# Tile 2 transposed within contraction step 1, in two parts, and multiplied ahead of step 2

## The chip, the cores and the metric

The kernel runs on one core of one Trainium2 chip. The metric is the device time of one execution in microseconds (us). Every run in this document was of the fast state with a listed clock of 1.0; where two kernels are compared by a ratio, it is the mean time of one kernel's fast runs over that of the other's of the same rounds, so it is not quite the ratio of the medians that are quoted.

Engines are named as the profile names them: PE is TensorE's matmul side, PEld its weight loads, ACT is ScalarE, DVE is VectorE, POOL is GpSimd, SP issues most of the DMA transfers. PSUM (PS in the profile's lines) is the memory into which PE writes here; an eviction is the copy of a result out of it. A load lands when its last part has arrived, and a hole is a stretch in which PE has nothing to start.

## The reference, cut to what matters

The input is 2048 rows of 512 numbers. They are layer-normalized, and the result goes into two branches whose outputs are added to the input: a state space model and a gated feed-forward net. The change touches only the first matmuls of the second branch, for the first 512 rows.

```python
x = A_x                                  # (1, 2048, 512), bf16
xn = _layernorm(x, axis=-1)
return x + _A_ref(xn, ...) + _B_ref(xn, w_gate, w_up, w_down)

def _B_ref(x, w_gate, w_up, w_down):     # 512 -> 1376 -> 512
    return (_gelu(x @ w_gate) * (x @ w_up)) @ w_down
```

## The kernel before

The kernel is a list of operations, each with an engine, a modelled duration, and the tiles that it reads and writes. A static scheduler orders ACT, DVE and POOL from the model; PE and SP keep the order in which the program names their operations. The order on PE is therefore what the source says.

At the start nothing is on the chip, so the first 512 rows are worked off in the order in which data arrive. They form four tiles of 128 rows (0 to 3). Each is centred on DVE, transposed on PE in blocks of 128 columns into PSUM (`cent_T`), and evicted by ACT. The contraction over 512 columns has four steps (k = 0 to 3). Each step needs a slice of the gate weights and a slice of the up weights, which come as separate loads in the order of the steps, with the rows of tiles 2 and 3 between them. `ks(k, j, ...)` multiplies step k of tile j.

```python
def cent_T(j, k0, k1, bank, eng="A", c0=0):   # transpose blocks k0..k1 of tile j, then evict
    ...
    PE(f, 56.0 * (k1 - k0), [XNp[j][k0 > 0] if j < 2 else XN[j], IDN], [BANK[bank]], "T0")
    ...
def GT_k(k, j, u, ws, first=False):           # one matmul of step k, tile j, column group u
    ...
    PE(lambda e: e.matmul(dst, XCd(j, k), WGU[:, ws[0]:ws[-1] + 1, k, f0:f1], ...),
       ..., [(WGc, WUc)[w_][k] for w_ in ws] + [XCs[j][k > 0]] + ..., [BANK[bank]], "GK")
...
def ks(k, j, w_, first=False):
    for u in range(2):
        GT_k(k, j, u, w_, first)
...                                           # step 0 of tiles 0 and 1, their transposes
for j in range(2):
    ks(1, j, [0, 1])                          # step 1 of tiles 0 and 1
ch(*stats(0, 2)); ch(sub(2)); ...             # DVE: centre tile 2
...
cent_T(2, 0, 4, 7)                            # all of tile 2, one eviction
for j in range(2):
    ks(2, j, [0, 1])                          # step 2 of tiles 0 and 1
for k in range(3):
    ks(k, 2, [0, 1], k == 0)                  # steps 0, 1, 2 of tile 2
for j in range(3):
    ks(3, j, [0, 1])                          # step 3 of tiles 0, 1, 2
    ...
    if j == 0:
        cent_T(3, 0, 4, 6)
for (j, u), bank in zip([(3, 0), (3, 1), ...], ...):
    GT_mm(j, u, bank)                         # tile 3 over all steps, and the rest
```

## Time and profile before

| | before |
|---|---|
| time, first three runs | 177.21, 177.51, 178.35 us; median 177.51 us |
| span of the profiled execution | 175.7 us |
| PE busy | 172.1 us of it |
| idle PE just ahead of step 2 | 0.25 us (7.18 to 7.42) |
| tile 3's first matmul over all steps | 11.10 us |

From the page of before: the busy time of PE, and the shares of the chain that ended last.

```profile
PE 172.1 (98%) x868; PEld 84.0 (48%) x883; DVE 159.8 (91%) x279; ACT 95.5 (54%) x185; POOL 10.7 (6%) x24
...
PE 98%; issue 1%; DVE 0%
```

PE bounds the kernel from beginning to end. A busy share says little about what can be won; the starts of the matmuls say more. The timeline of PE in before, where the columns are start, time until the group ended, engine, line, operation, shapes and count (L679 are transposes, L700 the matmuls of single steps, L711 tile 3):

```profile
4.57 0.38 PE L700 MATMUL PS<-arena 128*128 128x256 bf16 x2
...
4.84 0.38 PE L700 MATMUL PS<-arena 128*128 128x256 bf16 x2
...
5.77 1.35 PE L700 MATMUL PS<-arena 128*128 128x256 bf16 x6
6.95 0.39 PE L679 MATMUL PS<-arena 128*128 128x128 bf16 x4
7.42 2.75 PE L700 MATMUL PS<-arena 128*128 128x512 bf16 x12
10.01 0.39 PE L679 MATMUL PS<-arena 128*128 128x128 bf16 x4
10.23 1.03 PE L700 MATMUL PS<-arena 128*128 128x512 bf16 x4
11.10 0.81 PE L711 MATMUL PS<-arena 128*128 128x512 bf16 x3
```

The end of a matmul in the profile reaches into the next one (one of 512 columns is shown as 0.38 us long, and the next starts 0.216 us after it), so holes have to be read from starts. Four transposes start at 6.95 and should have been followed by a matmul at 7.18 (four times 0.056 us); the next starts at 7.42. The trace has the landing of step 2's up slice at 7.29, and the matmul follows 0.135 us after it. That is the hole that the change aims at. From 7.42 on, matmuls of 512 columns start every 0.2157 us without a gap. Fifteen holes of exactly one matmul's length later in the trace are lost records: the page has 868 matmuls beside 883 weight loads.

One more line of before matters later. It is the view of one line's instructions (L700) between 4.4 and 6.4 us, with shortest, middle and longest duration in ns:

```profile
L700 PE MATMUL PS<-arena x10: 270/272/377, 4.6 to 6.3; 128*128 128x256 bf16 x8, 128*128 128x512 bf16 x2
```

A matmul of 256 columns takes about 0.27 us in this execution from its first real matmul on.

### The profile page before, as it was taken

What the parts mean: (1) busy time and instruction counts of PE and PEld (TensorE: products, weight loads), DVE (VectorE), ACT (ScalarE), POOL (GpSimd) and SP (SyncE); (2) the same over time, 40 slices, a digit from 0 to 9 for tenths busy, and PEclk for the clock granted to TensorE, in tenths of its full rate; (3) what the DMA queues carried; (4) which work ended last, traced back from release to release, by engine and by line L of the source; (5) the groups of instructions that cost most, each with busy time, mean ns of one, the idle gap of its engine ahead of it and who ended that gap; (6) DMA issues with size and microseconds to landing.
All of it is one profiled execution on the core that took longest, in us unless ns stands there. A gap on an engine that the chain in (4) does not pass through costs nothing.

```text
span 175.7 us, 2494 instructions
## 1 busy us (share of the span) xinstructions
PE 172.1 (98%) x868; PEld 84.0 (48%) x883; DVE 159.8 (91%) x279; ACT 95.5 (54%) x185; POOL 10.7 (6%) x24
## 2 busy tenths in 40 slices
PE   8999999999999999999999999999999999999995
PEld 3545564644544444444644444444464444444454
DVE  6987999996999989889899999989999899999941
ACT  5476677899876898383576792000667970000000
POOL 3122030201000000002100000000000000000000
DMA  5899999695998000002015000002001000000311
GB/s 155 241 320 174 215 178 222 126 132 113 191 298 225 0 4 2 0 30 85 8 39 111 1 0 0 4 0 90 30 0 30 4 0 0 0 0 0 120 64 60
DMA packets 32420, 14.36 MB, mean 82 GB/s; under 512 B 23736, under 2 KB 32408, under 8 KB 32408
## 3 DMA queue, kind: packets, MB, share of 16 engines
q1 hardware_dynamic: 32240, 14.07, 35.5%
q8 instruction: 7, 0.11, 0.3%
q10 hardware_dynamic: 168, 0.13, 0.2%
q14 instruction: 5, 0.04, 0.1%
HBM read 6.46 MB, written 2.10 MB: 49 GB/s over the span
## 4 chain that ended last, share of the span: by engine, by line
PE 98%; issue 1%; DVE 0%
PE PS L883 37%; PE PS L842 32%; PE PS L748 16%; PE PS L711 4%; PE PS L700 3%; PE PS L816 3%; PE PS L932 2%; PE PS L679 1%; PE PS L939 0%; DVE arena L901 0%
## 5 line engine op out<-in xcount | busy, mean ns | idle before, releaser
L883 PE MATMUL PS<-arena 128*128 128x512 bf16 (+3 forms) x317 | 65.9, 366 | 0.3
L842 PE MATMUL PS<-arena 128*128 128x512 bf16 x257 | 57.1, 379 | 0.4
L883 PEld LDWEIGHTS PS<-arena 128*128 128x128 bf16 (+1 forms) x323 | 30.8, 98 | 35.2
L842 PEld LDWEIGHTS PS<-arena 128*128 128x128 bf16 x264 | 25.8, 98 | 30.2
L786 DVE TENSOR_TENSOR_SCAN arena<-arena 128x512 bf16<-128x512 f32 x32 | 38.9, 1255 | 0.0
L857 ACT ACTIVATE arena<-PS 128x512 bf16<-128x512 f32 x33 | 19.8, 599 | 25.8 <-DVE arena L901 16.7
L748 PE MATMUL PS<-arena 128*128 128x512 bf16 (+1 forms) x134 | 28.0, 366 | 0.1
L861 ACT ACTIVATE arena<-PS 128x512 bf16<-128x512 f32 x33 | 19.8, 600 | 5.1 <-PE PS L842 5.1
L875 ACT ACTIVATE PS<-arena 128x512 f32<-128x512 bf16 (+2 forms) x17 | 9.6, 581 | 19.7 <-DVE arena L901 19.0
L748 PEld LDWEIGHTS PS<-arena 128*128 128x128 bf16 x136 | 13.3, 98 | 14.1
L757 ACT ACTIVATE arena<-PS 128x512 bf16<-128x512 f32 x32 | 17.7, 592 | 2.1 <-PE PS L748 2.1
L901 DVE TENSOR_TENSOR arena<-PS,arena 128x512 bf16<-128x512 f32 (+2 forms) x17 | 10.9, 653 | 6.4 <-PE PS L883 6.4
L863 DVE TENSOR_TENSOR arena<-arena 128x512 bf16<-128x512 bf16 x33 | 13.1, 416 | 1.7 <-ACT arena L861 1.6
L775 DVE TENSOR_TENSOR arena<-arena 128x4096 bf16<-128x4096 bf16 (+1 forms) x5 | 9.2, 1859 | 0.8 <-ACT arena L606 0.8
L773 DVE TENSOR_TENSOR arena<-arena 128x4096 bf16<-128x4096 bf16 (+1 forms) x5 | 9.2, 1859 | 0.1
L798 DVE TENSOR_TENSOR arena<-arena 128x4096 bf16<-128x4096 bf16 x4 | 9.2, 2288 | 0.1
L799 DVE TENSOR_TENSOR arena<-arena 128x4096 bf16<-128x4096 bf16 x4 | 9.1, 2284 | 0.0
L720 ACT ACTIVATE arena<-PS,arena 128x256 bf16<-128x256 f32 (+1 forms) x16 | 6.6, 448 | 3.9 <-PE PS L700 2.1
L610 DVE BATCH_NORM_STATS2 arena<-arena 128x6 f32<-128x512 bf16 x12 | 7.7, 679 | 0.1
L711 PE MATMUL PS<-arena 128*128 128x512 bf16 (+1 forms) x40 | 7.1, 336 | 0.0
L723 DVE SCALAR_TENSOR_TENSOR arena<-PS,arena 128x256 bf16<-128x256 f32 (+1 forms) x16 | 6.3, 445 | 0.5 <-PE PS L700 0.5
L700 PE MATMUL PS<-arena 128*128 128x512 bf16 (+1 forms) x28 | 6.2, 349 | 0.2
(96 smaller groups left out, 124.6 us busy)
## 6 DMA issues: line engine op xcount, KB each, us to landing
out_dram<-arena SPq DMA_DIRECT2D x15, 128.0 KB, 1.7
arena<-in_A_x_dram SPq DMA_DIRECT2D x3, 512.0 KB, 5.3
arena<-in_B_w_down_dram SPq DMA_DIRECT2D x1, 1280.0 KB, 7.2
arena<-in_B_w_gate_dram SPq DMA_DIRECT2D x4, 128.0 KB, 3.0
arena<-in_B_w_up_dram SPq DMA_DIRECT2D x4, 128.0 KB, 3.1
arena<-in_B_w_gate_dram SPq DMA_DIRECT2D x1, 480.0 KB, 6.5
arena<-in_B_w_up_dram SPq DMA_DIRECT2D x1, 480.0 KB, 7.4
arena<-arena SPq DMA_TRANSPOSE x25, 3.1
```

The source lines that it names most:

```text
L700: PE(lambda e: e.matmul(dst, XCd(j, k), WGU[:, ws[0]:ws[-1] + 1, k, f0:f1], start=first, stop=k == KD - 1, skip_group_check=True), d_pe([w ...
L711: ins_ = e.matmul(dst, XCd(j, k), WGU[:, :, k, f0:f1], start=(k == 0), stop=(k == KD - 1))
L748: ins_ = e.matmul(PS[bank][:, 128 * j0:128 * j1], BBT[c][dk].ap[:, 128 * s:128 * (s + 1)], XNT[b].ap[:, dk, 128 * j0:128 * j1], start=(dk ...
L757: GATE["evBu"] = ACT(lambda e, bank=bank, k3=k3, s=s, c=c: e.activation(SSc[k3][s][c].ap, PS[bank][:, :], ACTF.Copy), d_act(512), [BANK[ba ...
L786: V(lambda e, g=g, rb=rb, init=init: e.tensor_tensor_scan(g.ap, rb, g.ap, init, ALU.mult, ALU.add), d_dve_scan(512), [g, PA[RRr]] + ([CARc ...
L842: ins_ = e.matmul(PS[bank][0:m, c0:c1], W.ap[:, dk, 128 * ft:128 * ft + m], XNT[b].ap[:, dk, c0:c1], start=(dk == 0), stop=(dk == KD - 1))
L857: GATE["last_gelu"] = ACT(lambda e, bg=bg, kk=kk, m=m: e.activation(GG[kk].ap[0:m, :], PS[bg][0:m, :], ACTF.Gelu_apprx_tanh), d_act(512), ...
L861: ACT(lambda e, bu=bu, kk=kk, m=m: e.activation(UPB[kk].ap[0:m, :], PS[bu][0:m, :], ACTF.Copy), d_act(512), [BANK[bu]], [UPB[kk]], "evU")
L863: V(lambda e, kk=kk, m=m, ft=ft, k2=k2: e.tensor_tensor(HTt[k2][ft].ap[0:m, :], GG[kk].ap[0:m, :], UPB[kk].ap[0:m, :], ALU.mult), d_dve_tt ...
L875: ACT(lambda e: e.activation(PS[bank][:, c0:c1], X[tt].ap[:, c0:c1], ACTF.Copy), d_act(c1 - c0), [X[tt]], [BANK[bank]], "seed")
L883: ins_ = e.matmul(PS[bank][:, c0:c1], l_[:, 128 * j:128 * (j + 1)], r_[:, c0:c1], start=False, stop=last and n == len(ops) - 1, skip_group ...
L901: V(lambda e: e.tensor_tensor(OUTB[ko].ap[:, c0:c1], PS[bank][:, c0:c1], XD[tt].ap[:, c0:c1], ALU.add), d_dve_1x(c1 - c0), [BANK[bank], XD ...
```

## The change

The intent is to have something to multiply while step 2's weights are on their way. Tile 2 is transposed earlier, between step 1 of tile 0 and step 1 of tile 1, in one block and three, so that the first block is evicted early. Its steps 0 and 1, four matmuls of 0.2157 us or 0.86 us, then run ahead of step 2. The number of matmuls and transposes stays the same; one ACT eviction is added. The last two edits only exchange two PSUM banks for the transposes and matmuls of tile 3.

```diff
         ks(0, 1, [1])
-        for j in range(2):
-            ks(1, j, [0, 1])
-        ch(*stats(0, 2)); ch(sub(2)); ch(*stats(0, 0)); ch(*stats(0, 1))
+        ch(*stats(0, 2)); ch(sub(2))
+        ks(1, 0, [0, 1])
+        cent_T(2, 0, 1, 7)
+        cent_T(2, 1, 4, 6)
+        ks(1, 1, [0, 1])
+        ks(0, 2, [0, 1], True)
+        ch(*stats(0, 0)); ch(*stats(0, 1))
...
-        cent_T(2, 0, 4, 7)
-        for j in range(2):
+        ks(1, 2, [0, 1])
+        for j in range(3):
             ks(2, j, [0, 1])
-        for k in range(3):
-            ks(k, 2, [0, 1], k == 0)
...
-                cent_T(3, 0, 4, 6)
+                cent_T(3, 0, 4, 7)
...
-                                (7, 6, 0, 1, 2, 3, 4, 5, 0, 7)):
+                                (6, 7, 0, 1, 2, 3, 4, 5, 0, 7)):
```

## The prediction

> **What bounds the kernel.** TensorE. The page has it busy 172.1 of 175.7 us; the chain of waits is 98% PE. The timeline of PE starts shows no real gap after 7.42 us: matmuls follow every 0.216 us (512 columns) or 0.108 us (256)[...]. The 15 later holes of 0.216 us ("issue" in the chain) are lost records: 868 matmuls stand beside 883 weight loads, 15 apart. So only PE idle time before 7.5 us can be won.
>
> **That idle time.** Between the last fill matmul (4.24) and 7.42: 0.27 us (first eviction by DVE), 0.15 (eviction of tile 1's block 0), 0.07 (step 1's weights and an eviction), 0.02 (tile 1's second eviction), and 0.25 from 7.18 to 7.42: tile 2's transposes are done, and step 2 waits for its up-weight slice, which lands at 7.29 (landing to next matmul start: 0.135 us).
>
> **What the change does.** Matmul and transpose work is the same. Tile 2's transposes split into 1 + 3 blocks between tile 0's and tile 1's step 1; tile 2's steps 0 and 1 (four matmuls, 0.86 us) move ahead of step 2. Added: one ScalarE eviction (0.28 + 0.49 us in place of 0.60) at about 6.75 us, where ScalarE idles 0.9 us. DVE's order is chained and the same.
>
> Expected PE times:
> - step 1 of tile 0: 6.06 as now; transposes of tile 2 at 6.49 (its centred rows are ready at 6.19).
> - step 1 of tile 1: 6.71; tile 2 step 0: 7.14 (block evicted by about 7.08); tile 2 step 1: 7.58.
> - step 2 of three tiles: 8.01 to 9.31, without waiting: its weights landed at 7.29.
> - step 3: its up slice lands at 9.25, so the first matmul cannot start before 9.39. It would have been ready at 9.31; before, it started at 9.58. So 0.07 to 0.1 us of the win becomes a new wait here.
> - from then on the order is as before, 0.19 us earlier. Tile 3's eviction must end by about 10.85; ScalarE does the first gelu just ahead of it, so 0 to 0.05 us may be lost.
>
> Of the 0.27 us removed, about 0.15 to 0.19 us remains, all on the critical path. Nothing downstream has less slack: the second weight chunk lands 0.9 us, the first B matrix 0.7 us, the transposed tiles 0.7 to 0.8 us before their first matmul.
>
> **Predicted time.** 177.51 - 0.2 = 177.3 us; range 176.8 to 177.9, as the three runs of before spread over 1.1 us. Chances: faster by over 2% 0.01, within 2% 0.98, slower 0.01. With repeated rounds I expect a ratio of about 0.999.
>
> **What would show it.** The PE timeline: the 0.25 us hole before step 2 gone; step 3 starting within 0.15 us of its up slice's landing, with a wait on a DMA there; tile 3's first matmul at about 10.9 instead of 11.10 us; later work shifted by as much; matmul count unchanged but for lost records.
>
> **What would make it wrong.** (1) The landing of the step 3 slices moves from run to run; 0.2 us later, the win is nil, since before too would then sit on it; earlier, up to 0.27 us. (2) The kernel's static scheduler reorders ScalarE, DVE or GpSimd; that could open a PE wait later, which the chain would show. (3) The split eviction comes later than 7.14, if ScalarE is busy: a hole before tile 2's step 0 or 1.

## The result, and the profile after

The changed kernel took 177.5 us (median of six runs, 177.25 to 177.98), the kernel before 177.41 us (six runs, 177.21 to 178.35). The ratio is 1.000 with a 95% interval of 0.9975 to 1.0025. The time lies in the predicted range, but the predicted gain of 0.2 us is not to be seen: the interval is 0.44 us wide to each side, and a change without any effect would have met the range too.

The order of instructions on DVE, POOL and SP is the same in both programs; on ACT one eviction became two, and PE has the new order. So the static scheduler did not disturb anything else.

From the page of after, the same two lines:

```profile
PE 172.8 (98%) x868; PEld 84.5 (48%) x883; DVE 159.8 (91%) x279; ACT 95.6 (54%) x186; POOL 10.7 (6%) x24
...
PE 98%; issue 0%; DVE 0%
```

PE is busy 0.7 us longer, with the same number of matmuls. The span is 176.2 us, 0.5 us longer than in the profile of before. The timeline of PE in after shows where that comes from:

```profile
4.73 0.59 PE L700 MATMUL PS<-arena 128*128 128x256 bf16 x2
...
5.21 0.63 PE L700 MATMUL PS<-arena 128*128 128x256 bf16 x2
...
6.61 0.82 PE L700 MATMUL PS<-arena 128*128 128x256 bf16 x4
7.27 0.39 PE L679 MATMUL PS<-arena 128*128 128x128 bf16 x4
7.49 3.19 PE L700 MATMUL PS<-arena 128*128 128x512 bf16 x14
10.51 0.39 PE L679 MATMUL PS<-arena 128*128 128x128 bf16 x4
10.74 1.03 PE L700 MATMUL PS<-arena 128*128 128x512 bf16 x4
11.60 0.38 PE L711 MATMUL PS<-arena 128*128 128x512 bf16 x1
```

Two things are to be read here. First, the hole is gone: from step 1's first matmul (6.84, within the group of 6.61) to tile 3 (11.60) there is 4.76 us, which is just the work, 20 matmuls of 0.2157 us and 8 transposes of 0.0557 us. In before the same stretch took 5.04 us (6.06 to 11.10). (PE came later here; by the estimate under experiments 1 and 2 the old order would have had no hole at step 2 in this execution either.) Second, step 1 begins 0.78 us later than in before, although the code up to there is the same in both kernels. Of these, 0.16 us are there from the first transpose on (4.03 against 3.87 us; the first rows landed that much later, at 2.97 against 2.82 us). The rest comes after it: the first two pairs of matmuls took 0.59 and 0.63 us, against 0.38 us in before. The view of line L700 in after, between 4.4 and 6.4 us:

```profile
L700 PE MATMUL PS<-arena x6: 373/421/421, 4.7 to 6.2; 128*128 128x256 bf16 x6
```

These matmuls ran at half speed until about 6.5 us; in before, full speed was there at 4.2 us. The starts show the step. In both traces the dummies of 512 columns ahead of the real work start every 0.427 us (1.15 to 3.28 us), and from step 1 on matmuls of 512 columns start every 0.216 us when nothing holds them, so the first rate is half of the second. At 128 columns the starts are 0.107 us apart before the step and 0.056 us after it: in after three transposes start at 6.386, 6.493 and 6.553 us, in before three dummies at 4.058, 4.164 and 4.238 us. I call this step the opening of TensorE's clock. It came at different times under identical code; what sets its moment was not shown. In after's trace the record of the granted clock, which no view prints, begins at 6.49 us as well; before's trace has none. The profile page does not show the opening: after's row of the granted clock reads full speed from the first slice, and the page of before has no such row.

The clock is not the only thing that makes step 1 late. In after, step 1's up slice landed at 6.46 us (5.84 in before), so step 1 could not have begun before 6.46 at any speed: at least 0.40 of the 0.78 us would have come from the loads alone.

So comparing these two profiles' spans would compare two openings of the clock (4.2 and 6.5 us) and two sets of landings, not two orders. Everything after tile 3's first matmul took the same time in both: 162.509 us to the start of the last matmul. What the change can do is done before that point.

### The profile page after: what moved, and what is told of

Its sections match the earlier page's. It is cut to its first block, busy times and chain, and to the rows that moved or that the text cites. A ratio compares the mean times of both kernels' runs of the same rounds, so it can differ in the third digit from the quotient of the medians.

```text
span 176.2 us, 2495 instructions
## 1 busy us (share of the span) xinstructions
PE 172.8 (98%) x868; PEld 84.5 (48%) x883; DVE 159.8 (91%) x279; ACT 95.6 (54%) x186; POOL 10.7 (6%) x24
## 3 DMA queue, kind: packets, MB, share of 16 engines
HBM read 6.46 MB, written 2.10 MB: 49 GB/s over the span
## 4 chain that ended last, share of the span: by engine, by line
PE 98%; issue 0%; DVE 0%
PE PS L883 37%; PE PS L842 32%; PE PS L748 16%; PE PS L711 4%; PE PS L700 3%; PE PS L816 3%; PE PS L932 2%; PE PS L679 1%; PE PS L939 0%; DVE arena L901 0%
## 5 line engine op out<-in xcount | busy, mean ns | idle before, releaser
L842 PE MATMUL PS<-arena 128*128 128x512 bf16 x257 | 57.1, 379 | 0.4
L842 PEld LDWEIGHTS PS<-arena 128*128 128x128 bf16 x264 | 25.8, 98 | 30.2
L748 PE MATMUL PS<-arena 128*128 128x512 bf16 (+1 forms) x134 | 28.0, 366 | 0.1
L901 DVE TENSOR_TENSOR arena<-PS,arena 128x512 bf16<-128x512 f32 (+2 forms) x17 | 10.9, 653 | 6.4 <-PE PS L883 6.4
L711 PE MATMUL PS<-arena 128*128 128x512 bf16 (+1 forms) x40 | 7.1, 336 | 0.0
L700 PE MATMUL PS<-arena 128*128 128x512 bf16 (+1 forms) x28 | 6.8, 379 | 0.0
```

The costliest lines, as they stand in the source:

```text
L711: ins_ = e.matmul(dst, XCd(j, k), WGU[:, :, k, f0:f1], start=(k == 0), stop=(k == KD - 1))
L748: ins_ = e.matmul(PS[bank][:, 128 * j0:128 * j1], BBT[c][dk].ap[:, 128 * s:128 * (s + 1)], XNT[b].ap[:, dk, 128 * j0:128 * j1], start=(dk ...
L842: ins_ = e.matmul(PS[bank][0:m, c0:c1], W.ap[:, dk, 128 * ft:128 * ft + m], XNT[b].ap[:, dk, c0:c1], start=(dk == 0), stop=(dk == KD - 1))
L901: V(lambda e: e.tensor_tensor(OUTB[ko].ap[:, c0:c1], PS[bank][:, c0:c1], XD[tt].ap[:, c0:c1], ALU.add), d_dve_1x(c1 - c0), [BANK[bank], XD ...
```

## The experiments

The theory (A): the hole that the change removes exists only when PE comes early to step 2, ahead of its weights. When the clock opens late, or the weights of steps 0 and 1 are late, PE comes late and finds the weights there; then there is nothing to win. The first profile of before was an early case. Rival B: the new order gives back what it saves (split eviction, earlier need of tile 2, a new wait before step 3). Rival C, tested in one pair: the gain does not depend on when PE arrives.

All twelve kernels gave correct results except two.

### 1 and 2. Both kernels again, unchanged

No edit.

> The kernel before, unchanged, against itself. Theory A (the moment at which TensorE's clock opens differs from run to run, and hides the change): ratio 1.000 within 0.003, single times spread over 0.5 to 1.2 us, and in this profile the clock opens at another time than the 4.2 us seen in the first profile of before; if it opens after about 5 us, the hole before step 2 is shorter than 0.25 us. Rival B (the new order costs what it saves): the clock opens at 4.2 us again and the hole is 0.25 us.

> The changed kernel, unchanged, once more. Both theories: ratio 0.997 to 1.003. Theory A: if the clock opens at 4 to 5 us here, the first matmul of tile 3 over all steps starts at 10.9 us (11.10 in the first profile of before); if it opens at 6 us or later, at 11.4 us or later.

The kernel before against itself: 177.26 us (six runs), ratio 0.9988 (0.9971 to 1.0005). The changed kernel: 177.29 us (six runs), ratio 0.9989 (0.9966 to 1.0012). A kernel differs from itself by as much as the change was predicted to give. (The expected spread of single times, 0.5 to 1.2 us, was a miss for these six runs of before: 177.08 to 177.40.) The timeline of PE in the second profile of before:

```profile
4.63 0.58 PE L700 MATMUL PS<-arena 128*128 128x256 bf16 x2
...
6.39 1.38 PE L700 MATMUL PS<-arena 128*128 128x256 bf16 x6
7.60 0.39 PE L679 MATMUL PS<-arena 128*128 128x128 bf16 x4
7.82 2.75 PE L700 MATMUL PS<-arena 128*128 128x512 bf16 x12
...
11.50 0.38 PE L711 MATMUL PS<-arena 128*128 128x512 bf16 x1
```

Here the clock opened at about 6.1 us (0.58 us for the first pair; three transposes took 0.52 us from 5.54 on, and 0.33 us from 6.22 on), PE came to step 2 at 7.82, and step 2's up slice had landed at 7.57. Four transposes from 7.60 to 7.82 are followed at once by the matmuls: the old order, with no hole, and 4.76 us from step 1 (6.74) to tile 3. In this execution the change had nothing to remove.

The second profile of after was an early one by the clock (full speed by 4.65 us: 0.38 us for the first pair), but the weights were late:

```profile
5.36 0.39 PE L700 MATMUL PS<-arena 128*128 128x256 bf16 x2 [0.28 <-DMA arena<-in_B_w_up_dram]
...
7.06 0.40 PE L679 MATMUL PS<-arena 128*128 128x128 bf16 x4
7.29 3.18 PE L700 MATMUL PS<-arena 128*128 128x512 bf16 x14
...
11.40 0.38 PE L711 MATMUL PS<-arena 128*128 128x512 bf16 x1
```

Step 0's up slice landed at 5.32 instead of 4.63 (a wait of 0.28 us named in brackets, 0.44 us by the starts), and step 1 began at 6.59. The expectation of tile 3 at 10.9 us was a miss: it started at 11.40. It had assumed that the loads land as in the first profile.

From the traces one can work out an estimate of what the other order would have done in the same execution. Take the start of step 1, the landings of the slices of steps 2 and 3 plus 0.135 us, the end of ACT's eviction of tile 1, and the durations of matmul and transpose above. The old order reaches step 2 after 1.09 us of work, the new one after 1.95 us, 0.86 us later. For the executed order this sum gives the start of tile 3 within 0.001 us in nine of the ten profiles with unchanged weights. In the tenth, the second profile of after, it is 0.048 us too early, since tile 2's transposes waited there for their centred rows, which the sum leaves out. The gain is the difference between the executed order's own start of tile 3 and the sum for the other order. For the four profiles of the two kernels as they are:

| profile | full speed from | step 1 starts | step 2's up slice lands | step 1 to tile 3 | gain of the new order (estimate) |
|---|---|---|---|---|---|
| before, first | 4.2 us | 6.06 | 7.29 | 5.04 us | 0.19 us |
| before, second | 6.1 us | 6.74 | 7.57 | 4.76 us | 0.00 us |
| after, first | 6.5 us | 6.84 | 7.43 | 4.76 us | 0.08 us |
| after, second | by 4.65 us | 6.59 | 7.66 | 4.81 us | 0.07 us |

The mean is 0.09 us, 0.05% of the time. The 0.08 us of the third row is not the hole at step 2 but the wait for tile 1's eviction, which tile 2's transposes cover.

### 3 and 4. Full clock before the first load, with dummy matmuls ahead of it

```diff
+        hold = PE(lambda e: [e.matmul(PS[4][:, :], ...) for _ in range(20)][-1], ...)
-        ld_x0(0)
+        ld_x0(0, "sync", [hold])
-        ... ld_x0(1, "scalar", [wrm]) ...
+        ... ld_x0(1, "scalar", [wrm, hold]) ...
-            for _ in range(nwarm):        # 7
+            for _ in range(14):
```

> The kernel before with 20 dummy matmuls put ahead of the first load, so that the clock is open before any real work (7 to 8 us longer than before, ratio 1.04). Both theories: full speed from the first real matmul, a hole of 0.2 to 0.3 us before step 2, as in the first profile of before.

> The changed kernel with the same 20 dummy matmuls. Theory A: with the clock open throughout it beats the held version of before by 0.15 to 0.28 us (median time and the time from the first real matmul to the first of tile 3 over all steps), with a short DMA wait before step 3. Rival B (split eviction and the later wait give back what the hole gave): less than 0.05 us apart.

Measured: 184.29 us (183.57 to 185.06) for the held version of before, 184.73 us (184.57 to 185.1) for the held version of after. By time, the expectation of a gain was a miss: the held version of after was even 0.44 us slower in the median. The timeline of PE in the held version of before:

```profile
14.61 0.39 PE L679 MATMUL PS<-arena 128*128 128x128 bf16 x4
15.51 2.75 PE L700 MATMUL PS<-arena 128*128 128x512 bf16 x12 [0.52 <-DMA arena<-in_B_w_up_dram]
...
19.18 7.09 PE L711 MATMUL PS<-arena 128*128 128x512 bf16 x40
```

And in the held version of after:

```profile
14.05 0.39 PE L679 MATMUL PS<-arena 128*128 128x128 bf16 x4
14.27 3.19 PE L700 MATMUL PS<-arena 128*128 128x512 bf16 x14
...
18.38 7.09 PE L711 MATMUL PS<-arena 128*128 128x512 bf16 x40
25.96 3.40 PE L842 MATMUL PS<-arena 128*128 128x512 bf16 x15 [0.48 <-DVE arena L723]
```

The clock was open: the first pair of real matmuls took 0.38 us in both (from 12.22 and 12.13 us). Full speed came while the dummies ran; whether they brought it about, no run tested. With the clock open, before has a hole of 0.68 us ahead of step 2 (from 14.83 to 15.51; 0.2 to 0.3 us were expected), and the wait is named as the up slice's load. The held version of after has none: 4.76 us from step 1 to tile 3, against 5.48 us. So the stretch itself went as theory A says, except that the expected wait before step 3 did not come. But the times do not follow. The dummies started at half speed and ended at full speed, and the step came at another time in each: between 5.0 and 6.5 us PE has five matmuls in the profile of before and six in that of after, between 6.5 and 8.0 us eight and nine. So the hold's own length differs between runs (the first load was issued at 8.14 us in the profile of before, at 7.93 in that of after). And in the profiled run of after 0.43 us were lost later, at the first L842 group (25.96). The wait is put down to DVE there. PE's queue had been held until 25.64 by the landing of the last transposed input tile at 25.61, which comes at 24.47 in the other kernel's profile, so I take the landing for the cause. From step 1 to the last matmul 0.28 of the 0.72 us are left in the two profiles. The pair is inconclusive as to time.

### 5 to 8. The hold timed by DVE, and PE delayed by half a microsecond

The first hold's length differed with the clock (8.14 and 7.93 us). In these four kernels the loads wait for seven scans on DVE instead, while 27 dummies run on PE; the late versions have nine dummies of 128 columns more, ahead of step 1. (The second batch of dummies, 14 long, waits for the scans too.)

```diff
+        timer = V(lambda e: [e.tensor_tensor_scan(TB..., TA..., ...) for i in range(7)][-1], ..., [TA], [TB], 'timer')
-        ld_x0(0)
+        ld_x0(0, "sync", [timer])
...
-        ks(0, 1, [1])
+        ks(0, 1, [1]); fill(9, 0.0)       # late versions only
```

> The kernel before, held back by a chain of seven scans on DVE (about 9 us)[...]; all loads and the second batch of dummies wait for the last scan. Against the first held pair the delay no longer depends on when the clock opens, so single times should spread less than 1 us. Theory A and rival B: full clock from the first real matmul, a hole of 0.25 to 0.7 us before step 2, until the up slice has landed.

> The changed kernel held back in the same way. Theory A (with the clock open, the change removes the hole before step 2, less a wait of up to 0.2 us before step 3): median 0.15 to 0.6 us below that of the held version of before, and no hole over 0.2 us between step 1 and tile 3's matmuls. Rival B (the new order gives back what it saves even with the clock open): within 0.1 us of it.

> The held kernel before, with nine dummy matmuls of 128 columns (0.50 us) in front of step 1, so that PE comes to step 2 half a microsecond later, as it does when the clock opens late. Theory A: the hole before step 2 shrinks by up to 0.5 us, and the kernel grows by only 0.0 to 0.25 us over the held one. Rival B: the same for this kernel.

> The held changed kernel with the same nine dummies. Theory A: it has no hole to fill, so it grows by 0.35 to 0.5 us over the held one, and its gain over the late version of before falls to between 0 and 0.15 us: arriving late at step 2, before has nothing left that the change could take. Rival C (the gain does not depend on when PE arrives): the gain stays what it was without the dummies.

| kernel | median (runs) | step 1 to tile 3, profiled run | tile 3 to last matmul |
|---|---|---|---|
| timed, before | 186.46 us (186.21 to 186.78) | 4.84 us | 163.515 us |
| timed, after | 186.39 us (186.20 to 186.57) | 4.87 us | 163.215 us |
| timed and late, before | 186.39 us (186.18 to 186.89) | 4.76 us | 162.589 us |
| timed and late, after | 186.07 us (185.86 to 187.11) | 4.76 us | 163.460 us |

The expected gain of 0.15 to 0.6 us in the first pair was a miss (0.07 us between the medians, which is within the 0.1 us that rival B foresaw), for two reasons that the profiles show. In the profiled run of before, the weights of step 2 landed 1.03 us behind the start of step 1 (1.23 us in the first profile of before), so the hole in before was only 0.05 us; and in after step 3's up slice landed late and cost 0.12 us of the foreseen new wait. After was no early case either: PE stood 0.40 us ahead of step 1 (14.58 to 14.98), whose up slice landed at 14.89, and the sum above gives the same start of tile 3 for both orders. Then both lost time further on. The first L842 group in the timed version of before, and in the timed version of after:

```profile
27.84 1.46 PE L842 MATMUL PS<-arena 128*128 128x512 bf16 x6 [0.83 <-DMA arena<-arena]
```

```profile
27.49 1.89 PE L842 MATMUL PS<-arena 128*128 128x512 bf16 x8 [0.55 <-DVE arena L723]
```

In these held kernels PE runs ahead of the transposes of the input by DMA and of DVE's evictions, which in the kernels as they are have slack there (in the first four profiles the last tile landed 1.2 to 1.8 us ahead of its first matmul). A gain of some tenths can be swallowed by that later wait. The timeline of PE at step 2 in the late version of before (14 to 20.6 us), and then in the late version of after:

```profile
16.39 0.39 PE L679 MATMUL PS<-arena 128*128 128x128 bf16 x4
16.61 2.75 PE L700 MATMUL PS<-arena 128*128 128x512 bf16 x12
```

```profile
15.92 0.39 PE L679 MATMUL PS<-arena 128*128 128x128 bf16 x4
16.15 3.19 PE L700 MATMUL PS<-arena 128*128 128x512 bf16 x14
```

In the late pair PE comes to step 2 after its weights in both orders, and both take 4.76 us for the stretch: arriving late leaves nothing to win, as theory A says. But the pair does not refute rival C, since the pair without the extra dummies showed no gain in the stretch either (4.84 and 4.87 us), and by time the late pair differs by more (0.32 us between the medians, against 0.07), not by less as theory A expected. Against rival C stand the holes of the old order instead: 0.25 us and none in the two profiles of before, 0.68 and 0.05 us in its held and timed versions. As to growth by the dummies, the times can't tell: they spread over 1.25 us in one of the kernels, and the expected growth of 0.35 to 0.5 us in the last one did not show. Its profiled run also lost 0.84 us at 42.4 us, which I have not followed up.

### 9 and 10. Step 2's weights made late on purpose

The jitter of the loads (step 1's up slice landed at 5.72 to 6.46 us in the first four profiles) hides an effect of 0.1 us, so this pair makes the effect large. The loads of the slices of steps 2 and 3 are exchanged in the queue, so that step 2 needs what lands last. The results stay correct, and the order on every engine stays that of the kernel it derives from.

```diff
+        PLACE = (0, 1, 3, 2)
-            e.dma_start(W.ap[:, k, f0:f1], src[128 * k:128 * (k + 1), f0:f1])
+            e.dma_start(W.ap[:, PLACE[k], f0:f1], src[128 * PLACE[k]:128 * (PLACE[k] + 1), f0:f1])
...                                           # after scheduling: the matmuls of steps 2 and 3
+                op.deps = [other.get(d.id, d) for d in op.deps]   # wait for the exchanged loads
```

> The kernel before, with the loads of the step 2 and step 3 weight slices exchanged in the queue (same steps, same results, same order on every engine). In the profiles so far the last slice lands 1.1 to 2.2 us after the one before it, so step 2 now waits for it: a hole of 1.0 to 2.2 us before step 2, none before step 3, and a time 1.0 to 2.0 us above before.

> The changed kernel with the same exchange. Theory A (tile 2's steps 0 and 1, 0.86 us of matmuls, cover up to 0.86 us of lateness of the step 2 weights; in the unchanged kernel there is just too little lateness to cover): its hole before step 2 is 0.86 us shorter, and it is 0.6 to 0.9 us faster than the swapped version of before. Rival B (the new order gives back what it covers): within 0.3 us of it.

Measured: 178.85 us for the swapped version of before (ratio to before 1.0078, 1.0061 to 1.0095), 178.01 us for the swapped version of after (1.0030, 1.0013 to 1.0048), six runs each on the same chip. Their mean times differ by 0.84 us (178.745 less 177.907), with a standard error of 0.15 us worked out from the twelve times. Both expected times were met. (The 1.1 to 2.2 us of the first expectation are 1.07 to 2.36 us in the ten traces.) The timeline of PE in the swapped version of before:

```profile
7.43 0.39 PE L679 MATMUL PS<-arena 128*128 128x128 bf16 x4
8.79 2.75 PE L700 MATMUL PS<-arena 128*128 128x512 bf16 x12 [0.98 <-DMA arena<-in_B_w_up_dram]
```

And in the swapped version of after:

```profile
7.38 0.39 PE L679 MATMUL PS<-arena 128*128 128x128 bf16 x4
7.60 3.28 PE L700 MATMUL PS<-arena 128*128 128x512 bf16 x14
```

Before waits 1.14 us (7.65 to 8.79, while the last slice lands at 8.66). In after the matmuls of tile 2 fill that time, and 0.10 us of waiting is left within the group of fourteen. That is 1.04 us less rather than 0.86, as the two executions differ in the start of step 1 (6.57 and 6.95 us) and in the landings. When step 2's weights are late, the new order gains as much as its four extra matmuls take, 0.86 us, within the error. Rival B, that the new order gives back what it covers, falls. This pair is the one in which the effect stands clear of the noise.

### 11 and 12. No wait for the weights of steps 2 and 3

Steps 2 and 3 are multiplied by step 1's slice, which is there; the result is wrong (relative error 0.32).

```diff
-    ... WGU[:, ws[0]:ws[-1] + 1, k, f0:f1] ...            [(WGc, WUc)[w_][k] for w_ in ws]
+    ... WGU[:, ws[0]:ws[-1] + 1, min(k, 1), f0:f1] ...    [(WGc, WUc)[w_][min(k, 1)] for w_ in ws]
```

> The kernel before with steps 2 and 3 multiplied by the slice of step 1, which is there already (wrong result on purpose): neither step waits for a load. Theory A: no hole before step 2 and step 3, 4.76 to 4.86 us from step 1 to tile 3's matmuls, but hardly faster than before, 0.0 to 0.25 us, since the hole is worth only about 0.1 us in an average run.

> The changed kernel with the same wrong slices. Theory A: with nothing to wait for, the two orders are the same to within 0.1 us (4.76 to 4.82 us from step 1 to tile 3's matmuls). Rival B: the new order has a cost of its own, and without waits it is 0.1 us or more slower than the other.

The timeline of PE (6.8 to 11.5 us) at step 2 and at tile 3 in the first, and then in the second:

```profile
7.53 2.75 PE L700 MATMUL PS<-arena 128*128 128x512 bf16 x12
...
11.29 0.38 PE L711 MATMUL PS<-arena 128*128 128x512 bf16 x1
```

```profile
7.16 3.19 PE L700 MATMUL PS<-arena 128*128 128x512 bf16 x14
...
11.34 0.38 PE L711 MATMUL PS<-arena 128*128 128x512 bf16 x1
```

Measured: 177.74 us (ratio 1.0020, 1.0002 to 1.0039) and 177.44 us (1.0017, 0.9991 to 1.0043). In the profiles, step 1 (6.45 and 6.50 us) to tile 3 takes 4.839 us in the one and 4.838 us in the other: without waits for these weights the two orders took the same in the profiled runs, and the new order showed no cost of its own. (Both have 0.08 us of idle PE just ahead of tile 3. Tile 3's eviction, which the prediction feared there, had ended 0.14 us before in both, and what held PE was not followed up.) The expectation that the first is up to 0.25 us faster than before was a miss: it was 0.2% slower. In its profiled run a later line shows a loss:

```profile
19.30 1.89 PE L842 MATMUL PS<-arena 128*128 128x512 bf16 x8 [0.92 <-ACT arena L720]
```

PE idled 0.87 us there. The wait is put down to ACT, but PE's queue was held until 18.97 by the last transposed input tile, which landed at 18.95; in the other profiles of kernels without a hold it landed between 16.9 and 17.3. Why these transposes were late in this run, and whether that also made the other runs of this kernel slow, stays open.

## Why the prediction was right or wrong, point by point

- **The time and the class** were right: 177.5 us lies in 176.8 to 177.9, within 2% of before. This says nothing for the mechanism, as before's own 177.41 us lies there too. The forecast ratio of 0.999 can't be told from the measured 1.000 (0.9975 to 1.0025), nor from the 0.9988 of before against itself.
- **PE as the bound and the lost records**: right. 162.509 us from tile 3 to the last matmul came out the same, to 0.001 us, in the four profiles of the unchanged kernels, so no later wait appeared or went there.
- **What the change removes**: right as a mechanism, wrong as a size. The prediction says "Of the 0.27 us removed, about 0.15 to 0.19 us remains, all on the critical path." The term that was mis-sized is the 0.25 us hole. It was read from one execution and taken as fixed; in the second profile of before it was 0.00 us, in the held version 0.68 us. The estimates over four profiles give 0.00 to 0.19 us for the gain, with a mean of 0.09 us.
- **The cause that was missing** from its list of what could go wrong: when PE comes to step 2. The list named the landing of step 3's slices only. The runs showed that full speed came anywhere from 4.2 to 6.5 us in the four profiles, and that the up slice of step 0 landed at 5.32 instead of 4.63 us in one, that of step 1 at 5.72 to 6.46 us. In the second profile of before the late clock closed the hole (full speed from 6.1 us, PE at step 2 at 7.82, the slice there at 7.57). In the second profile of after a late load delayed PE, and in the first one a load would have held step 1 until 6.46 us even at full speed.
- **The new wait before step 3**: it appeared in one profile (0.12 us in the timed version of after), and not in the two profiles of after as it is, where PE arrived later and step 3 did not wait. There it was right only for the early case that it was worked out for.
- **The split eviction**: right. In after, ACT did it in 0.66 us for both parts, hidden behind step 1 of tile 1 and step 0 of tile 2. Only in the second profile of after did the earlier need of tile 2 cost anything, 0.03 us ahead of its transposes.
- **The static scheduler**: the feared reordering did not come.
- **The marks to look for**: the hole gone, yes, but the estimate has it gone in the first profile of after under the old order too; tile 3 at 10.9 us, no (11.60 and 11.40 us), because PE began step 1 later in both profiles.

What is settled: the new order covers up to 0.86 us of lateness of step 2's weights (0.84 us measured when they were made late), and showed no cost of its own in the pair without waits. What the kernel as it is gains from it on average, 0.09 us by estimate, no timing here resolves. No version was found that beats both kernels clear of noise.

## What to carry to other kernels

Before you spend work on a hole that one profile shows, take a second profile of the same kernel: a hole that depends on a race between an engine and a load may be absent in the next execution, as here (0.25 us in the first profile of before, none in the second). Compare two profiles from a point that the change affects to a point behind it, not span with span, when something ahead of it differs from run to run. When an effect is smaller than the noise, make its cause larger on purpose (here, late weights): that tests the mechanism, and the size in the plain kernel can then be estimated from the landings in its traces.

## What else the traces showed

- As far as two profiles of before can show it, the opening of the clock helps to decide whether loads are waited for. In them full speed came at 4.2 and 6.1 us; PE was done with tile 2's transposes at 7.18 and 7.82 us, step 2's up slice landed at 7.29 and 7.57 us, and the wait was 0.25 us in the early run and none in the late one. So the size of the hole was not the same in two executions of one kernel.
- In this kernel every matmul of the stream has its own weight load (883 loads beside 868 recorded matmuls), and where nothing holds them the starts are 0.2157 us apart at 512 columns and 0.0557 us at 128 (transposes).
- The profile's row of the granted clock did not show the late opening: in after it read full speed from the first slice, while matmuls of 256 columns took 0.42 us instead of 0.27 us and the trace's first record of the granted clock begins at 6.49 us. In before there are no records and no row.
- Weight loads move between executions of one kernel. For the same 128 KB slice and the same place in the queue, the landing of step 0's up slice was 4.63, 4.69, 4.71 and 5.32 us in four profiles, and that of step 3's 8.74 to 9.61 us.
